# The first 256 tokens as two blocks of 128, the low halves of eight weight chunks through one PSUM bank, and joint maxima of two heads

## The chip, the cores and the metric

The kernel runs on one core of one Trainium2 chip. The metric is the device time of one execution in microseconds. The kernel before took 636.36 us, the median of three runs from 635.49 to 637.52. Beside these stands one more execution, recorded by the profiler, from which all rows below come: 633.81 us, with a span of 632.0 us from its first to its last instruction.

## The reference

Attention with rotated queries and keys, and behind it two matrix products with a bent line between them. Batch 4, 8 heads, 576 tokens, 64 columns a head; then 2304 tokens of 512 columns, 2048 hidden.

```python
def rotate(x):
    x1, x2 = (x[..., :half], x[..., half:])
    return np.concatenate([x1 * cos - x2 * sin, x1 * sin + x2 * cos], axis=-1)
q_rot, k_rot = (rotate(q), rotate(k))
scores = 1.0 / np.sqrt(D) * np.matmul(q_rot, k_rot.transpose(0, 1, 3, 2))
attn = np.exp(scores - np.max(scores, axis=-1, keepdims=True))
attn = attn / (np.sum(attn, axis=-1, keepdims=True) + 1e-09)
x = np.matmul(attn, v)      # heads side by side: 2304 x 512
h = x @ w_in                # 2304 x 2048
g = np.where(h >= 1, h, np.where(h <= -1, 0.0, (h + 1) ** 2 / 4.0))
return g @ w_out            # 2304 x 512
```

The weights come to the kernel as float64 words, q, k and v as float32.

## The kernel before

**Numbers.** Every operand of a matmul is held as two fp16 tiles, a high half and a low half (the rest after rounding). A product is the sum of three: high by high, high by low, low by high (TERMS). The high half is one ScalarE copy, the low half one VectorE instruction that multiplies, subtracts the high half and rounds.

**Attention.** Tokens of a batch go in tiles of 128; a batch has four such tiles and 64 tokens left over. An item is one tile of one pair of heads. For each item TensorE writes the scores of the two heads, 576 columns each, into psS0 and psS1 (L582, 12 matmuls; two PSUM banks each). VectorE takes the maximum of each (L556), ScalarE the exponential with its sum (L558), ScalarE and VectorE scale the sums and take the reciprocal (L561, L563), ScalarE writes the high half of the probabilities (L566) and VectorE the low half (L568). One transposing DMA from SP's queue turns both halves of both heads (phl to pT). When two items of a head pair have landed, 28 matmuls multiply 256 tokens with the values and write psV (L611): the high half of V (vS), the chunk left over and the halves mixed for it (vM, which three DMAs fill from vS), the low half, and zeros (vZ). Two head pairs fill the bank; ScalarE and VectorE read it into the high and low half of xT (L626, L629). After four head pairs the 256 tokens are ready for the MLP. The 64 tokens left over go the same way in items of their own (L594), into xL, and those of two batches make one MLP block of 128 tokens.

**MLP.** A block of 256 tokens takes eight steps. A step is two groups of 12 matmuls of 256 columns into psH (L692), ScalarE's clipped copy a (L699), r and g on VectorE and ScalarE (L702 to L713), and 12 matmuls of 512 columns that add to psO0 and psO1, one bank for each 128 tokens (L722). A block of 128 tokens takes four steps of four groups of 12 at 128 columns and 12 matmuls into one of the two banks. In the first three blocks (ACT_BLOCKS) ScalarE takes over one VectorE instruction in each step.

**Preparation.** Per batch the rows of K and Q are loaded twice (the second time with the halves of the columns swapped), turned with three VectorE instructions (L341, L343, L345), and split. V is scaled with a factor that a root gives: TensorE sums columns with a matmul against ones (L311), and a few small VectorE instructions follow. The weights come in eight chunks of w_in and eight of w_out, 1 MB each. A chunk is decoded by three VectorE instructions (L506, L508, L510) into a float32 scratch of 128 x 1024, which is in turn xT1 and the output tile o; ScalarE writes the high half (L519). For the first five chunks of both (PE_CHUNKS) the low half is made on TensorE, in two half chunks of 512 columns: the scratch through the identity (L535) and minus the high half (L536) into psO0 for the first half chunk and psO1 for the second, from where ScalarE writes it (L539). For the last three it is one VectorE instruction (L527).

**Order.** A planner fixes the order of each engine ahead of time. Each step has a cost in ns, a place in the program and the buffers that it reads and writes; the due times of TensorE's steps go back through what they need, a table SLACK shifts groups of steps and single ones, and the planner lets each engine take, of the steps that are ready by its own clock, the one that is due first. The engines then run their lists in order and wait on semaphores. Loads and transposes stand in SP's list, the later weight chunks in GpSimd's.

## Time and profile before

| | |
|---|---|
| median of three runs | 636.36 us (635.49 to 637.52) |
| profiled execution | 633.81 us, span 632.0 us |
| TensorE busy | 559.8 us, 89% of the span |
| VectorE busy | 511.2 us, 81% |
| ScalarE busy | 441.0 us, 70% |
| GpSimd busy | 7.5 us, 1% |
| read from HBM | 40.96 MB, 72 GB/s with the writes |

Three more kinds of view are used below. A window gives each engine's busy time in a stretch. A timeline gives the rows of one engine in order, with the idle time ahead of a row and what ended it in brackets; the recorded lengths of neighbouring rows overlap a little, so the time that an instruction takes from its engine is read from start to start. A list of waits sums such idle time by the instruction that waited and by what it waited for. A name as psO stands for both tiles of that name in these views.

### The profile page before, as it was taken

The page shows a single profiled execution, that of the slowest core. Times are in us where ns is not written, and L with a number is a line of the kernel's source. Part 1 is how long each engine was busy: PE and PEld are TensorE (multiplying, and loading weights), DVE is VectorE, ACT ScalarE, POOL GpSimd, SP SyncE. Part 2 cuts the span into 40 slices and gives each one's busy share as a digit, 9 for nine tenths or more (in the row PEclk, how much of TensorE's full clock was granted, in tenths as well). Part 3 has the DMA queues.
Part 4 walks back from the last instruction along what each step waited for, and adds up shares of the span by engine and source line. Part 5 has one row for each costly group of instructions (what it writes and reads, how often), then busy time and mean ns, then how long its engine had stood idle before and what let it go on. Part 6 is the DMA issues. An engine that isn't in the chain of part 4 may idle for free.

```text
span 632.0 us, 12652 instructions
## 1 busy us (share of the span) xinstructions
PE 559.8 (89%) x5078; PEld 358.6 (57%) x5078; DVE 511.2 (81%) x839; ACT 441.0 (70%) x881; POOL 7.5 (1%) x18
## 2 busy tenths in 40 slices
PE   1346678799997999999998999999999999999995
PEld 1112234566654666666665676676666676666663
DVE  5998999999999999998897889889877874333422
ACT  3647898978999799984878798877787663232221
POOL 0000100000000000000000000000000000000000
PEclk9997879999998999999999999999999999999999
DMA  8997988695699858876377765856666553000000
GB/s 265 372 305 261 258 231 161 133 233 132 142 260 203 195 99 188 205 164 161 92 163 129 124 127 109 136 94 115 113 131 129 85 99 77 1 8 27 1 34 18
DMA packets 188011, 91.33 MB, mean 145 GB/s; under 512 B 170160, under 2 KB 178608, under 8 KB 185904
## 3 DMA queue, kind: packets, MB, share of 16 engines
q1 hardware_dynamic: 186224, 77.94, 56.0%
q0 software_dynamic: 1728, 12.58, 5.6%
q8 instruction: 40, 0.66, 0.4%
q14 instruction: 19, 0.16, 0.1%
HBM read 40.96 MB, written 4.72 MB: 72 GB/s over the span
## 4 chain that ended last, share of the span: by engine, by line
PE 56%; DVE 22%; DMA 12%; ACT 6%; issue 3%; SPq 0%; ACTq 0%
PE psO L722 21%; PE psH L692 21%; PE psV L611 7%; PE psS L582 5%; DMA pT<-phl 5%; DVE phl L568 4%; DVE mx L556 3%; DMA rk<-in_km_dram 3%; DMA vM<-vS 2%; ACT p L558 2%; DVE g L713 1%; ACT phl L566 1%; DMA rv<-in_vm_dram 1%; DVE r L709 1%; DVE xT L508 1%
## 5 line engine op out<-in xcount | busy, mean ns | idle before, releaser
L722 PE MATMUL psO<-w,g 128*128 128x512 f16 x864 | 211.7, 380 | 1.9 <-ACT g L711 0.9
L692 PEld LDWEIGHTS <-w 128*128 128x128 f16 x1920 | 170.9, 98 | 44.4 <-issue 5.2
L692 PE MATMUL psH<-xT,w 128*128 128x256 f16 x1536 | 187.7, 273 | 3.2 <-ACT a L699 3.2
L558 ACT ACTIVATE p<-psS,mx 128x576 f32<-128x576 f32 x144 | 105.3, 733 | 26.1 <-DVE mx L556 20.1
L722 PEld LDWEIGHTS <-g 128*128 128x128 f16 x864 | 79.3, 98 | 75.2 <-DVE g L713 2.5
L568 DVE SCALAR_TENSOR_TENSOR phl<-p,sums,phl 128x576 f16<-128x576 f32 x144 | 113.4, 812 | 9.6 <-ACT phl L566 9.6
L566 ACT ACTIVATE phl<-p,sums 128x576 f16<-128x576 f32 x144 | 105.0, 765 | 17.5 <-DVE sums L563 15.2
L556 DVE TENSOR_REDUCE mx<-psS 128x1 f32<-128x576 f32 x144 | 104.3, 750 | 6.9 <-PE psS L582 6.2
L582 PE MATMUL psS<-kT,qT 64*128 64x512 f16 (+1 forms) x768 | 64.5, 295 | 22.6 <-ACT p L558 15.3
L711 ACT ACTIVATE g<-r 128x512 f16<-128x512 f32 x72 | 44.9, 624 | 47.5 <-DVE r L709 29.2
L699 ACT ACTIVATE a<-psH 128x512 f32<-128x512 f32 x72 | 42.4, 590 | 49.3 <-PE psH L692 48.7
L713 DVE SCALAR_TENSOR_TENSOR g<-r,g 128x512 f16<-128x512 f32 x72 | 49.5, 688 | 26.8 <-ACT g L711 26.7
L582 PEld LDWEIGHTS <-qT 64*128 64x128 f16 x768 | 31.2, 97 | 68.5 <-issue 47.9
L702 DVE SCALAR_TENSOR_TENSOR r<-a 128x512 f32<-128x512 f32 x48 | 33.1, 689 | 45.6 <-ACT a L699 45.2
L611 PE MATMUL psV<-pT,vS 128*64 128x256 f16 (+1 forms) x768 | 50.1, 253 | 3.8 <-DMA pT<-phl 3.5
L709 DVE SCALAR_TENSOR_TENSOR r<-a,r 128x512 f32<-128x512 f32 x72 | 49.6, 689 | 0.9
L611 PEld LDWEIGHTS <-vS 128*64 128x64 f16 x768 | 33.3, 112 | 18.5 <-issue 14.7
L611 PE MATMUL psV<-pT,vM 128*64 128x256 f16 (+1 forms) x480 | 29.2, 253 | 3.3 <-DMA vM<-vS 3.3
L558 ACT ACTIVATION_READ_ACCUMULATOR p<-psS,mx 128x1 f32 x144 | 28.1, 195 | 0.0
L692 PE MATMUL psH<-xL,w 128*128 128x128 f16 x384 | 25.5, 219 | 0.0
L611 PEld LDWEIGHTS <-vM 128*64 128x64 f16 x480 | 22.0, 113 | 4.1 <-DMA vM<-vS 3.8
L535 PE MATMUL psO<-xT,xL 128*128 128x512 f32 x20 | 15.4, 864 | 9.8 <-DVE xT L510 5.6
(98 smaller groups left out, 467.5 us busy)
## 6 DMA issues: line engine op xcount, KB each, us to landing
w<-in_w_in_dram POOLq DMA_DIRECT2D x5, 1024.0 KB, 6.9
rv<-in_vm_dram SPq DMA_DIRECT2D x8, 512.0 KB, 5.7
w<-in_w_out_dram POOLq DMA_DIRECT2D x4, 1024.0 KB, 7.3
out_dram<-o SPq DMA_DIRECT2D x16, 256.0 KB, 2.4
rq<-in_qm_dram SPq DMA_DIRECT2D x7, 512.0 KB, 7.2
dup<-in_qm_dram SPq DMA_DIRECT2D x7, 512.0 KB, 3.9
dup<-in_km_dram SPq DMA_DIRECT2D x6, 576.0 KB, 5.3
rk<-in_km_dram SPq DMA_DIRECT2D x6, 576.0 KB, 6.8
```

The lines of the kernel that those rows point to most:

```text
L556: plan.add("dve", dve_cost(S, psum=True), at, lambda m=m, src=src: nc.vector.tensor_reduce(out=m, in_=src, op=ALU.max, axis=AX.X, negate=T ...
L558: plan.add("act", act_cost(S, psum=True, ptrs=2), at, lambda a=a, e=e, m=m, src=src: nc.scalar.activation(out=p32[e], in_=src, func=AF.Exp ...
L566: plan.add("act", act_cost(S), at, lambda a=a, e=e, hi=hi: nc.scalar.activation(out=hi, in_=p32[e], func=AF.Copy, scale=rr[:, a:a + 1]), r ...
L568: plan.add("dve", dve_cost(S, ptrs=1), at, lambda a=a, e=e, hi=hi, lo=lo: nc.vector.scalar_tensor_tensor(out=lo, in0=p32[e], scalar=rr[:, ...
L582: nc.tensor.matmul(out=psS[a][:, lo:hi], lhsT=qT[hf][d, l, j, c:c + 128], rhs=kT[ks][d, j, m, lo:hi], start=z == 0, stop=z == 2)
L611: nc.tensor.matmul(out=outs[a], lhsT=st, rhs=moving(a, blk), start=z == 0, stop=z == len(seq) - 1)
L692: nc.tensor.matmul(out=psH[:, n * i:n * i + n], lhsT=wi[ft // 2][:, wl, kk, 128 * (ft % 2):128 * (ft % 2) + 128], rhs=xfn(xl, kk), start=z ...
L699: plan.add("act", act_cost(512, psum=True, ptrs=0), at, lambda one=one: nc.scalar.activation(out=a, in_=psH, func=AF.Relu, scale=2.0 ** -7 ...
L709: plan.add("dve", dve_cost(512), at, lambda one=one: nc.vector.scalar_tensor_tensor(out=r, in0=a, scalar=one, in1=r, op0=ALU.max, op1=ALU. ...
L711: plan.add("act", act_cost(512, ptrs=0), at, lambda g=g, one=one: nc.scalar.activation(out=g[:, 0], in_=r, func=AF.Relu, scale=1.0, bias=- ...
L713: plan.add("dve", dve_cost(512), at, lambda g=g, one=one: nc.vector.scalar_tensor_tensor(out=g[:, 1], in0=r, scalar=-one, in1=g[:, 0], op0 ...
L722: nc.tensor.matmul(out=psO[pos[tt]], lhsT=g[:, gl, n * i + 128 * tt:n * i + 128 * tt + 128], rhs=wo[ft // 2][:, wl, ft % 2, :], start=ft = ...
```

## The change

**Blocks.** The first 256 tokens of batch 0 are two blocks of 128 tokens. Each has four items, four value products of 128 columns that fill the psV bank together, one xT high half and one low half of 512 columns (L618, L621 in the new numbering, into the two halves of xT0), and an MLP block of four steps with groups at 128 columns. The later blocks stay at 256 tokens.

**Weights.** PE_CHUNKS goes from 5 to 8: the low halves of all eight chunks of w_in and of w_out are made on TensorE (L525, L526) and written by ScalarE (L529), and no chunk uses VectorE for it. That is 32 half chunks in place of 20. All of them use psO1 alone.

**Maxima.** psS0 and psS1 are the two halves of one tile. One VectorE instruction takes the maxima of both heads of an item (L545), 2 x 576 elements, in place of two; both exponentials wait for it. Items left over keep one head each.

**Plan.** ACT_BLOCKS goes from 3 to 4, which is the same 24 steps as before, since the first block has become two of four steps. The planner's costs of a score item, of value products and of the first loads change, and the SLACK table is another, so that the order of the whole program is another.

```diff
-    "k0.03 dve": -18_500, "k1 act": 68_700, "k1 dve": 128_000, "k1.12 dve": 2_700, "k1.20 dve": 192_800,
...
+    "k0 dve": 9_000, "k0.02 dve": 20_100, "k0.03 dve": 279_800, "k1 act": 69_500, "k1 dve": 575_900,
...
-PE_CHUNKS = 5
-ACT_BLOCKS = 3
+PE_CHUNKS = 8
+ACT_BLOCKS = 4
...
-    mx = [[sbt(f"mx{i}_{a}", [128, 1]) for a in range(2)] for i in range(4)]
+    mx = [sbt(f"mx{i}", [128, 2]) for i in range(4)]
...
-    psS = [ps.tile([128, 1024], F32, name=f"psS{i}") for i in range(2)]
+    psS_t = ps.tile([128, 2048], F32, name="psS")
+    psS = [psS_t[:, 1024 * i:1024 * i + 1024] for i in range(2)]
...
-                nc.tensor.matmul(out=psO[e], lhsT=idn, rhs=y[:, cut], start=True, stop=False)
-                nc.tensor.matmul(out=psO[e], lhsT=ndg[which], rhs=hi[:, cut], start=False, stop=True)
+                nc.tensor.matmul(out=psO[1], lhsT=idn, rhs=y[:, cut], start=True, stop=False)
+                nc.tensor.matmul(out=psO[1], lhsT=ndg[which], rhs=hi[:, cut], start=False, stop=True)
...
+        srcs = psS_t.rearrange("p (a s) -> p a s", a=2)[:, :, 0:S] if nh == 2 else psS[slot][:, 0:S]
+        plan.add("dve", dve_cost(nh * S, psum=True), at, lambda: nc.vector.tensor_reduce(
+            out=mx[ri][:, 0:nh], in_=srcs, op=ALU.max, axis=AX.X, negate=True),
+            r=[("psS", slot + a) for a in range(nh)], w=[("mx", ri)])
         for a, e in enumerate(es):
-            m, src = mx[ri][a], psS[slot + a][:, 0:S]
-            plan.add("dve", dve_cost(S, psum=True), at, lambda m=m, src=src: nc.vector.tensor_reduce(
-                out=m, in_=src, op=ALU.max, axis=AX.X, negate=True), r=[("psS", slot + a)], w=[("mx", ri, a)])
+            m, src = mx[ri][:, a:a + 1], psS[slot + a][:, 0:S]
...
-        xs = ring("xT", 2)
+        xs = 0 if n == 128 else ring("xT", 2)
+        c0 = 128 * ts[0] if n == 128 else 0
...
-                    dst = [xT[xs][:, l, :, 0:128] for l in range(2)]
+                    dst = [xT[xs][:, l, :, c0:c0 + 128] for l in range(2)]
...
-    blocks = [(b, ts, i == 1) for b in range(B) for i, ts in enumerate(([0, 1], [2, 3]))]
+    blocks = [(b, ts, ts[-1] == T - 1) for b in range(B) for ts in (([0], [1], [2, 3]) if b == 0 else ([0, 1], [2, 3]))]
+    counts["xT"] = 1
```

Three places of the new order, as the instruction lists of the two kernels show them; a number behind a name tells tiles apart.

VectorE ahead of the xT low half that completes the first block, in the kernel before (L629 writes it, for the second two head pairs of 256 tokens; L556 are maxima, L568 probability low halves, L508 and L510 decode a weight chunk into o or xT1):

```order
L556 TENSOR_REDUCE mx1_0_102<-psS0_112 128x1
L556 TENSOR_REDUCE mx1_1_103<-psS1_113 128x1
L568 SCALAR_TENSOR_TENSOR phl0_74<-p32_2_73,sums0_108,phl0_74 128x576
L508 SCALAR_TENSOR_TENSOR xT1_79<-w_61,xT1_79 128x1024
L629 SCALAR_TENSOR_TENSOR xT0_78<-psV_114,sca_99,xT0_78 128x512
L563 RECIPROCAL sums1_109<-sums1_109 128x2
L510 SCALAR_TENSOR_TENSOR xT1_79<-w_61,xT1_79 128x1024
```

and in the kernel after (L621 writes it, for four head pairs of 128 tokens; L545 is a joint maximum, L496 and L498 decode, L555 is the reciprocal):

```order
L555 RECIPROCAL sums2_106<-sums2_106 128x2
L545 TENSOR_REDUCE mx3_103<-psS_108 128x2
L496 TENSOR_SCALAR xT1_79<-w_61 128x1024
L621 SCALAR_TENSOR_TENSOR xT0_78<-psV_109,sca_99,xT0_78 128x4x128
L498 SCALAR_TENSOR_TENSOR xT1_79<-w_61,xT1_79 128x1024
L560 SCALAR_TENSOR_TENSOR phl0_74<-p32_0_71,sums2_106,phl0_74 128x576
```

This low half was instruction 171 of VectorE's list and is 140; the one of the second block is 184. The first turn of the next K (L341 before, L331 after), which was instruction 97, is 168.

TensorE at half chunks of the weights. The kernel before, among the scores of the first items (L535 the scratch through the identity, L536 minus the high half):

```order
L535 MATMUL psO0_116<-xT1_79,xL_80 128x512
L536 LDWEIGHTS xL_80
L536 MATMUL psO0_116<-w_61,xL_80 128x512
L535 MATMUL psO1_117<-xT1_79,xL_80 128x512
L536 LDWEIGHTS xL_80
L536 MATMUL psO1_117<-w_61,xL_80 128x512
```

and the kernel after, at one that stands inside the first MLP block (L685 is its psH group, L715 its product into psO0):

```order
L685 LDWEIGHTS w_61
L685 MATMUL psH_110<-xT0_78,w_61 128x128
L525 MATMUL psO1_112<-xT1_79,xL_80 128x512
L526 LDWEIGHTS xL_80
L526 MATMUL psO1_112<-w_61,xL_80 128x512
L715 LDWEIGHTS g0_83
L715 MATMUL psO0_111<-w_61,g0_83 128x512
```

Half chunks that took psO0 and psO1 in turn take psO1 each time. In the kernel before all 20 half chunks stand ahead of the first MLP matmul; now 15 stand ahead of it and 17 between it and the first MLP matmul of the second block.

TensorE at the first change of batch, where the root of the next V is taken (L311 before, L301 after, 128x3 into psV). The kernel before:

```order
L582 LDWEIGHTS qT0_64
L582 MATMUL psS1_113<-kT1_63,qT0_64 128x64
L311 MATMUL psV_114<-ssv_97,ones_95 128x3
L692 LDWEIGHTS w_61
L692 MATMUL psH_115<-xT1_79,w_61 128x256
```

and the kernel after:

```order
L715 LDWEIGHTS g1_84
L715 MATMUL psO1_112<-w_61,g1_84 128x512
L301 MATMUL psV_109<-ssv_97,ones_95 128x3
L715 LDWEIGHTS g0_83
L715 MATMUL psO0_111<-w_61,g0_83 128x512
```

The root stood behind the last left-over value product and a score item, with two MLP groups and their product behind it; it now stands between two MLP products, and more MLP steps stand between it and the next value product.

## Rows read from the trace of the kernel before

**Rows 1.** The slices of the profile's page: the busy share of TensorE and of VectorE, in tenths, in 40 equal slices of 15.8 us.
```profile
PE   1346678799997999999998999999999999999995
...
DVE  5998999999999999998897889889877874333422
```

**Rows 2.** Windows: a stretch, its length, the busy time of TensorE, of its weight loads, of VectorE, ScalarE and GpSimd in it (with instructions), the mean granted TensorE clock, the DMA share and GB/s.
```profile
0.00:108.70 108.70, 57.16 (x318) 26.85 (x318) 96.82 (x185) 74.67 (x147) 5.41 (x14) 0.92 0.90 266
108.70:186.00 77.30, 71.18 (x673) 46.97 (x668) 76.94 (x112) 67.83 (x131) 2.10 (x4) 1.00 0.76 179
186.00:209.00 23.00, 18.23 (x173) 11.41 (x172) 21.42 (x42) 20.19 (x41) 0.00 (x0) 0.85 0.97 214
```

**Rows 3.** Timeline of TensorE around the first MLP matmul: start, length by the record, line, operation, tiles.
```profile
105.52 1.13 PE L535 MATMUL psO<-o,xL 128*128 128x512 f32 x2
...
106.70 1.02 PE L535 MATMUL psO<-o,xL 128*128 128x512 f32 x2
...
107.87 0.91 PE L582 MATMUL psS<-kT,qT 64*128 64x512 f16 x12
108.71 2.79 PE L692 MATMUL psH<-xT,w 128*128 128x256 f16 x24
```

**Rows 4.** Timeline of VectorE at the turn of the next K (first row; in brackets the idle time ahead of it and what ended it), and ahead of the first MLP matmul.
```profile
50.47 1.36 DVE L341 TENSOR_TENSOR rk<-rk,rt 128x1152 f32<-128x1152 f32 x1 [2.60 <-DMA rk<-in_km_dram]
...
97.68 1.54 DVE L568 SCALAR_TENSOR_TENSOR phl<-p,sums,phl 128x576 f16<-128x576 f32 x2
99.13 1.42 DVE L556 TENSOR_REDUCE mx<-psS 128x1 f32<-128x576 f32 x2
100.46 0.68 DVE L506 TENSOR_SCALAR o<-w 128x1024 uint32<-128x1024 uint32 x1
...
101.67 1.22 DVE L508 SCALAR_TENSOR_TENSOR o<-w,o 128x1024 uint32<-128x1024 uint32 x1
102.80 0.16 DVE L563 RECIPROCAL sums<-sums 128x2 f32<-128x2 f32 x1
...
107.98 0.74 DVE L629 SCALAR_TENSOR_TENSOR xT<-psV,sca,xT 128x512 f16<-128x512 f32 x1
```

**Rows 5.** The chain that ended last, in order of time: start, length, engine, tile, line and instructions in a row. First from the stretch behind the first change of batch, then from the end.
```profile
210.69 1.30 PE psO L722 x6
...
214.22 1.65 PE psV L611 x28
...
217.27 1.31 PE psH L692 x12
...
607.37 1.34 PE psH L692 x24
...
624.15 2.35 PE psO L722 x10
```

**Rows 6.** Timeline of TensorE at the first change of batch: a left-over value product (its first of four rows, with the row behind the last), the column sums for the root of the next V, and the first use of a vM copy.
```profile
187.35 0.32 PE L611 MATMUL psV<-pT,vS 128*64 128x64 f16 x8
...
187.92 0.91 PE L582 MATMUL psS<-kT,qT 64*128 64x512 f16 x12
189.13 0.39 PE L311 MATMUL psV<-ssv,ones 128*128 128x3 f32 x2 [0.31 <-DVE xL L629]
...
202.13 1.28 PE L611 MATMUL psV<-pT,vM 128*64 128x256 f16 x10 [1.55 <-DMA vM<-vS]
```

**Rows 7.** Groups of instructions, different shapes apart: line, engine, operation, tiles, shapes and count; busy us and mean ns of one; idle time ahead of them and what ended it.
```profile
L692 PEld LDWEIGHTS <-w 128*128 128x128 f16 x1920 | 170.9, 98 | 44.4 <-issue 5.2
...
L558 ACT ACTIVATE p<-psS,mx 128x576 f32<-128x576 f32 x144 | 105.3, 733 | 26.1 <-DVE mx L556 20.1 <-DVE phl L568 4.3 <-PE psV L611 0.9
...
L556 DVE TENSOR_REDUCE mx<-psS 128x1 f32<-128x576 f32 x144 | 104.3, 750 | 6.9 <-PE psS L582 6.2 <-PE psS L594 0.6
...
L539 ACT ACTIVATE w<-psO,sca 128x512 f16<-128x512 f32 x20 | 13.1, 677 | 0.8 <-PE psO L536 0.8
...
L519 ACT ACTIVATE w<-xT,sca 128x1024 f16<-128x1024 f32 x8 | 9.1, 1143 | 5.3 <-DVE xT L510 4.1 <-DVE sca L328 1.1
...
L341 DVE TENSOR_TENSOR rk<-rk,rt 128x1152 f32<-128x1152 f32 x6 | 8.1, 1350 | 2.6 <-DMA rk<-in_km_dram 2.6
...
L527 DVE SCALAR_TENSOR_TENSOR w<-xT,sca,w 128x1024 f16<-128x1024 f32 x3 | 3.8, 1280 | 0.2 <-ACT w L519 0.2
...
L341 DVE TENSOR_TENSOR rk<-rk,rt 128x576 f32<-128x576 f32 x4 | 3.0, 755 | 0.0
```

**Rows 8.** What TensorE waited for: line and releaser, us in total, times, the longest. Three rows from 108 to 345 us, and the last one over the whole span.
```profile
PE psS L582 <- ACT p L558: 4.8, 7, 1.5
PE psV L611 <- DMA vM<-vS: 3.3, 2, 1.7
PE psH L692 <- ACT a L699: 3.2, 3, 1.5
...
PE psO L535 <- ACT w L539: 4.3, 5, 2.8
```

**Rows 9.** DMA issues: tile, queue, kind and count, median us from issue to landing.
```profile
pT<-phl SPq DMA_TRANSPOSE x80, 4.6
```

**Rows 10.** Windows of one engine: VectorE's busy time from the start to 232.8 us, and TensorE's from 232.6 us to its last matmul.
```profile
0.00:232.80 232.80, 218.77 (x369) 0.95 0.84 220
...
232.60:626.50 393.90, 389.62 (x3709) 1.00 0.50 101
```

More of the change, by code (lines that the diff above doesn't have):

```diff
@@ L292, in scalar, with dma @@
         return sca[:, nsca[0] - 1:nsca[0]], ("sca", nsca[0])
-    def dma(at, dst, src, r, w, nbytes, eng="sp", chain=[]):
+    def dma(at, dst, src, r, w, nbytes, eng="sp", chain=[], rate=320.0):
         q = nc.sync if eng == "sp" else nc.gpsimd
-        plan.add(eng, 600.0 if eng == "sp" else 1000.0, at, lambda: q.dma_start(out=dst, in_=src), r, w + chain, bw=nbytes / 400.0)
+        plan.add(eng, 600.0 if eng == "sp" else 1000.0, at, lambda: q.dma_start(out=dst, in_=src), r, w + chain, bw=nbytes / (rate if plan.group in ("init", "first") else 400.0))
     def dmaT(at, dst, src, r, w, nbytes):
```

89 lines of the change are left out of this document (39 added, 50 removed).

## The prediction

> **What bounds the kernel now.** I read the slices first [rows 1]: TensorE works a third of the time or less in the first 30 us and from some 110 us on nearly all of the time, with two slices of seven tenths; VectorE is full from the second slice to about the middle. So the kernel is TensorE's work behind a front in which VectorE feeds it too slowly. The windows give the sizes [rows 2]: ahead of 108.7 us TensorE is busy 57.2 us, partly at a reduced granted clock (0.92 in the mean), while VectorE is busy 96.8; behind it TensorE idles 6.1 of 77.3, then 4.8 of 23.0 (at a granted clock of 0.85). The edge at 108.7 is the first MLP matmul [rows 3]: it starts when the second xT low half of the first 256 tokens is done, which VectorE ends at the same moment.
>
> Prices are taken start to start. A VectorE instruction begins 0.08 ahead of the recorded end of the one before (101.67 plus 1.22 against 102.80) [rows 4], so each costs its row less 0.08. TensorE's pieces: one L692 group of 12 at 256 columns 1.31, at 128 columns 0.67, three L722 matmuls 0.65, a value product 1.65, for a left-over item 0.57, a score item 0.84, one half chunk through the identity 1.18 (105.52 to 106.70) [rows 3, 5, 6]. At these prices all of TensorE's pieces make 529.1 us. 40.4 lie ahead of 108.7, 488.7 behind.
>
> All differences are made on the profiled execution (633.81, span 632.0) and put on the median of the three runs, 636.36.
>
> **The change, part by part.**
>
> *Split first block.* The first MLP matmul now needs four items and four value products, not eight and four. The order has 19.9 us less on VectorE ahead of the xT low half that completes the first block: 20 single maxima (13.4) against 8 joint ones (10.2), 12 against 18 probability low halves (-4.4), 25 against 32 decode steps (-6.9), no turn of the next K (three of 1.27, -3.8), and 1.6 of small ones [rows 4, 7]. It also leaves out the one VectorE wait of size, 2.6 us for the next K at 50.47 [rows 4]: that turn now stands at row 168, some 45 us of VectorE work later, with its load issued before the first transposes. The first MLP matmul so moves from 108.7 to 108.7 - 19.9 - 2.6 = 86.2.
>
> *TensorE's added work.* 12 half chunks of 1.18 make 14.2. 64-column and 256-column value products give 0.57 and 1.65 and bound the 128-column one; on the line between them it is 0.93, so eight cost 7.4 in place of 6.6 (bounds 4.6 to 13.2). 32 MLP groups of 0.67 replace 16 of 1.31: 0.4. Sum +15.5 (544.6 in all); 29.1 of it lies ahead of the first MLP matmul, 515.5 behind. Start plus work behind goes from 108.7 + 488.7 = 597.4 to 86.2 + 515.5 = 601.7: **4.3 us worse, unless TensorE waits less behind that point.**
>
> *VectorE and ScalarE.* Six low halves (L527) leave VectorE, 1.20 each: -7.2. ScalarE takes 12 evictions of 0.68 less its overlap of 0.09: +7.1; it idles 34 us ahead of 108.7 and 9.5 in the 77 behind [rows 2], which hides them; without that cover they cost 7.1. No row shows a joint maximum. 576 more elements cost 0.595 (0.755 to 1.350) [rows 7], so it takes 0.75 + 0.595 = 1.345, 1.26 start to start, against 1.33 for a pair [rows 4]: 0.07 saved in each of 64. Bounds: 1.19 (no fixed part) and 1.42 (the pair's recorded length), -9.0 to +5.8 over the kernel, under half of that ahead of the point below. Its first exp starts 0.6 later; TensorE waited for an exp 7 times between 108 and 345 us [rows 8], so that is 0 to 4.2. I take 0, since those waits stand where the order has changed, and keep 4.2 for the range. The Trainium skill (VectorE: DVE Perf Modes, The TRN2 errata) gives a PSUM-source instruction a fixed 120 cycles at 0.96 GHz, 0.125 us: by it the 64 save 8.0 in place of 4.5. The pair that takes 1.33 in this trace speaks for less.
>
> *Queues.* SP's first 28 issues are the same. Then loads of K, Q and the three vM copies stand ahead of the first transposes, which wait for VectorE anyway; I cost it at nothing, covered by the 16 us of VectorE work between the fourth item's last low half and the xT behind it; without it a transpose's landing of 4.6 us [rows 9] is late. The half chunks share one bank: each waits for ScalarE's eviction of the one before, and TensorE's whole queue waits behind it. Ahead of 86 us TensorE has over 50 us to spare; behind it see the second rival.
>
> *Where the waits go.* After 108.7 TensorE has idle rows of 4.8 (exp), 3.3 (vM) and 3.2 us (ScalarE's read of psH) [rows 8]. The largest spot is the change of batch: at 189.13 the column sums for the root that scales the next V are taken, and TensorE stands on the last vM copy until 202.13 [rows 6]. That is 13 us, and in the order TensorE has 6.9 us of pieces there; its clock falls to 0.85 for the window [rows 2]. The new order has 19.5 us of pieces between that root and the next value product (18.2 against 16.1 at the second change of batch, 10.4 against 8.7 at the third). This spot should vanish.
>
> *What VectorE still allows.* At each MLP step and value product I added VectorE's work up to its input and TensorE's pieces from it on. The largest sum before is the 15th MLP step, 219.0 + 0.2 + 379.1 = 598.3; the window to 232.8 confirms the first number, 218.8 busy and 14.0 idle [rows 10]. The largest now is the 21st value product: 219.0 + 9.5 (eight more K and Q turns) - 7.2 (L527) - 0.5 (maxima) + 2.8 (two more low halves, one more MLP step, small ones) = 223.6, and 5.0 for transposing and landing, and 369.5 of pieces: 598.1. The sums are equal. So VectorE sets the pace up to there in both, and the change can win only in what lies above the sum.
>
> **The sum.** Before: TensorE takes from 232.6 to its end at 626.5 [rows 5, 10] 393.9 us for 379.1 of pieces, a factor of 1.039 that holds 4.3 us of idle time (393.9 less 389.6); 5.5 us of eviction and output follow. Now: 223.6 + 5.0 + 11.4 (14.0 idle less the 2.6) = 240.0, then 369.5 x 1.039 = 383.9, then 5.5: 629.4. If the idle time goes too: 625.2. I take the middle, 627.3, 4.7 under 632.0: **636.4 - 4.7 = 631.7 us**. By way of the first MLP matmul the end is 8.3 us earlier (74.1 of VectorE's work ahead of the first block's xT low half, 0.2 and 515.5 make 589.8 against 598.1): TensorE's slack in the front.
>
> **Rivals.** *No change.* VectorE waits for something else in the place of K and the waits at the change of batch turn up at another edge: the sums alone differ by 0.2, so 636.2. For it: ScalarE is busy 88% of the stretch behind 108.7 and gets more; against it: the longer cover at all three changes of batch.
>
> *Slower: the single bank.* Between the first MLP matmul and the second block's first one stand 47 us of pieces with 17 half chunks, one each 2.8 us. If ScalarE's eviction ends more than 1.6 us after the matmuls (2.8 - 1.2), TensorE stands. An eviction of 0.68 behind one exp (0.73) and one 1024-wide copy (1.14) [rows 7] ends after some 2.6 us: 17 x 1.0 = 17 us, less the slack of 8.3, is +8.7, and the time 640.4. It decides for slower from 2.5 us on. For it: ScalarE's queue is in order and full. Against it: with two banks the 20 half chunks of the present kernel waited for evictions five times, 4.3 us in all and 2.8 at the longest [rows 8]. At that rate 17 wait 3.7 us, inside the slack; only if most are like the longest does the rival come.
>
> *Narrow matmuls.* If the weight load of 98 ns [rows 7] set the pace of the 384 matmuls at 128 columns, they would cost 16.1 more, 7.8 after the slack: 639.5. Against it stand 24 such matmuls in 1.34 us, 56 ns each [rows 5], with the same weights. The Trainium skill (TensorE: Matmul & The Clock Gate, Back-to-back issue gap) has such pairs sustained at about 81 ns, a rule that speaks against narrow blocks; by it the change costs 9.6 more, 1.3 after the slack, and the time is 633.0. The row decides for 56.
>
> **How the numbers follow.** A measurement of this kernel can tell about 0.3%, 1.9 us, from no change. My forecast 0.57 (with its own range 626 to 634.4), no change 0.23, the single bank 0.14, narrow matmuls 0.03, more than forecast (VectorE's joint maxima at their lower bound) 0.03. Faster 0.58, same 0.23, slower 0.19. For 8 in 10 the range reaches down to 625 (joint maxima 2 better, all waits gone and less idle) and up to 640.5 (the single bank, or the waits for exps and value products of 1.65 together).
>
> **What will show it.** The first L685 matmul at 84 to 90 us; 12 of them at 128 columns in 0.67; a joint maximum of 1.30 to 1.40 us; VectorE idle 10 to 13 us ahead of 240; no wait for vM at the first change of batch; waits of L525 for ScalarE under 5 us behind the first MLP matmul. Wrong would be: TensorE idle over 12 us between 90 and 240, above all ahead of L525, or VectorE idle over 16 us in the same stretch.

## The result and the profile after

The changed kernel takes 643.09 us (median of eight runs, 640.88 to 647.68), the kernel before 635.30 in the same runs. The ratio is 1.0128 with a 95% interval of 1.0101 to 1.0155: 1.3%, some 8.1 us, slower. The profiled execution took 647.68 us, with a span of 645.9; it is the slowest of the eight, 4.6 us above their median, while the one of the kernel before stands 1.5 below its median. So 6 of the 13.9 us between the two traces are scatter and no part of the change; where that matters, the trace of e7 below stands beside it, a form of the changed kernel that took the same time and whose profiled execution (641.22 us) is nearer to the median. Of e5 and e9 below, some executions took over 1.5% longer than the fastest of the same kernel, and these are not compared.

The slices of the page, TensorE and VectorE, to lay beside [rows 1]:

```profile
PE   1238569989989999999989999999999999999996
...
DVE  6988689999999998999977888758668577634322
```

The windows up to the first MLP matmul, to the change of batch and over it (columns as in [rows 2]):

```profile
0.00:92.50 92.50, 43.21 (x267) 20.00 (x268) 76.42 (x150) 59.00 (x116) 4.54 (x13) 0.96 1.01 269
92.50:186.00 93.50, 85.59 (x922) 53.55 (x921) 89.64 (x121) 83.77 (x160) 2.64 (x5) 1.00 0.84 192
186.00:209.00 23.00, 21.90 (x244) 14.18 (x244) 22.73 (x37) 20.58 (x44) 0.00 (x0) 1.00 0.69 143
```

TensorE reaches the first MLP matmul at 92.5 us in place of 108.7, with 43.2 us of work behind it. From there to 186 us it idles 7.9 of 93.5, and over the change of batch 1.1 of 23.0 at full clock, where it had idled 4.8 at 0.85 [rows 2]. The timeline of TensorE, at the first value products, the first MLP matmul, and the first MLP groups behind it:

```profile
59.50 0.41 PE L603 MATMUL psV<-pT,vS 128*64 128x128 f16 x8
...
60.41 1.12 PE L525 MATMUL psO<-xT,xL 128*128 128x512 f32 x2
...
70.94 0.64 PE L603 MATMUL psV<-pT,vS 128*64 128x128 f16 x8 [4.59 <-DMA pT<-phl]
...
91.34 1.12 PE L525 MATMUL psO<-o,xL 128*128 128x512 f32 x2 [1.71 <-ACT w L529]
...
92.51 0.83 PE L685 MATMUL psH<-xT,w 128*128 128x128 f16 x12
...
104.49 1.50 PE L685 MATMUL psH<-xT,w 128*128 128x128 f16 x24
105.83 1.08 PE L525 MATMUL psO<-o,xL 128*128 128x512 f32 x2
```

A value product of 128 columns takes 0.91 (59.50 to 60.41), 24 matmuls of 128 columns 1.34 (104.49 to 105.83), 56 ns each. At 70.94 TensorE had stood 4.6 us on a transpose, and VectorE, one timeline down, 5.6 us on the scratch that TensorE had not yet read:

```profile
74.68 0.69 DVE L496 TENSOR_SCALAR o<-w 128x1024 uint32<-128x1024 uint32 x1 [5.64 <-PE psO L525]
...
91.37 0.74 DVE L621 SCALAR_TENSOR_TENSOR xT<-psV,sca,xT 128x512 f16<-128x512 f32 x1
```

The change of batch: the column sums for the root, and the only wait for vM up to 345 us.

```profile
199.26 0.28 PE L301 MATMUL psV<-ssv,ones 128*128 128x3 f32 x2
...
222.07 0.30 PE L603 MATMUL psV<-pT,vM 128*64 128x256 f16 x2 [0.57 <-DMA vM<-vM]
```

The groups with the joint maxima, the evictions of the half chunks, and the maxima of the items left over (columns as in [rows 7]):

```profile
L545 DVE TENSOR_REDUCE mx<-psS 128x2 f32<-128x1152 f32 x64 | 86.3, 1348 | 3.5 <-PE psS L574 3.4
...
L529 ACT ACTIVATE w<-psO,sca 128x512 f16<-128x512 f32 x32 | 21.8, 680 | 10.0 <-PE psO L526 9.5
...
L545 DVE TENSOR_REDUCE mx<-psS 128x1 f32<-128x576 f32 x16 | 11.8, 748 | 6.1 <-PE psS L586 5.3 <-ACT p L550 0.8
```

What TensorE waited for between 92 and 345 us, against [rows 8]. The waits for vM and psH are shorter than they were. Those of the score items are not: with the items left over (L586), which had no such wait there before, they sum to 5.4 us for exponentials and maxima, where it was 4.8. The wait of the half chunks is new in this stretch:

```profile
PE psO L525 <- ACT w L529: 5.8, 4, 1.9
PE psS L574 <- ACT p L550: 2.9, 3, 2.2
...
PE psH L685 <- ACT a L692: 1.8, 2, 1.1
PE psS L586 <- ACT p L550: 1.7, 4, 0.7
PE psS L586 <- DVE mx L545: 0.8, 1, 0.8
...
PE psV L603 <- DMA vM<-vM: 0.6, 1, 0.6
```

And behind 250 us, first the kernel before (its largest, and the only one of a score item), then the changed kernel (its three largest):

```profile
PE psV L611 <- DMA vM<-vS: 1.7, 1, 1.7
...
PE psS L582 <- ACT p L558: 0.4, 1, 0.4
```

```profile
PE psS L574 <- ACT p L550: 4.4, 5, 2.2
PE psS L586 <- ACT p L550: 3.1, 4, 1.2
PE psS L586 <- DVE mx L545: 1.4, 2, 0.8
```

There the score items wait for exponentials and maxima 8.9 us, where they waited 0.4. Half of it, 4.5 us, is of the items left over (L586).

**Where the time went.** The sum of the prediction was made up to one value product, the 21st (the 17th of the kernel before, for the same tokens). VectorE up to the low half that it waits for, before and after, and TensorE from it to the last matmul, before and after:

```profile
0.00:244.30 244.30, 229.78 (x389) 0.95 0.83 217
```

```profile
0.00:248.60 248.60, 227.14 (x355) 0.99 0.92 218
```

```profile
250.90:626.50 375.60, 371.79 (x3554) 1.00 0.49 99
```

```profile
253.30:641.30 388.00, 377.56 (x3590) 1.00 0.48 93
```

VectorE has 2.6 us less to do there (229.8 to 227.1) and idles 7.0 more (14.5 to 21.5). The value product starts at 253.3 instead of 250.9. From it on, pieces of 369.5 us are left instead of 365.5, and they take 388.0 instead of 375.6: 18.5 over the pieces instead of 10.1. That is 2.4 + 4.0 + 8.4 = 14.8 us to the last matmul; the eviction behind it is 0.9 shorter. The 4.0 are three MLP groups of 12 matmuls. In the trace of e7 VectorE idles 17.4, the product starts at 249.0 and TensorE then takes 385.8:

```profile
0.00:244.00 244.00, 226.64 (x355) 0.97 0.91 222
```

```profile
249.00:634.80 385.80, 377.46 (x3590) 1.00 0.48 93
```

That is -1.9 + 4.0 + 6.2 = 8.3, close to the difference of the medians. **VectorE's part is hardly faster, and behind it TensorE has more left and takes more than its pieces.**

### The profile page after: what moved, and what is told of

The parts are those of the page before. It is cut to its first block, busy times and chain, and to the rows that moved or that the text cites. A ratio compares the mean times of both kernels' runs of the same rounds, so it can differ in the third digit from the quotient of the medians.

```text
span 645.9 us, 13237 instructions
## 1 busy us (share of the span) xinstructions
PE 571.2 (88%) x5418; PEld 364.8 (56%) x5418; DVE 500.9 (78%) x769; ACT 446.5 (69%) x893; POOL 7.2 (1%) x18
## 4 chain that ended last, share of the span: by engine, by line
PE 40%; DVE 5%; DMA 5%; ACT 5%; issue 1%; SPq 0%; ACTq 0%; DVEq 0%
PE psO L715 17%; PE psH L685 16%; PE psS L574 3%; PE psV L603 3%; DMA pT<-phl 3%; ACT p L550 2%; DVE mx L545 1%; ACT phl L558 1%; DVE phl L560 1%; DMA rv<-in_vm_dram 1%; PE psS L586 1%; DMA dup<-in_qm_dram 1%; DVE r L702 0%; ACT g L704 0%; DVE vS L344 0%
## 5 line engine op out<-in xcount | busy, mean ns | idle before, releaser
L715 PE MATMUL psO<-w,g 128*128 128x512 f16 x864 | 213.8, 380 | 1.5 <-ACT g L704 0.9
L685 PEld LDWEIGHTS <-w 128*128 128x128 f16 x2112 | 175.6, 98 | 47.0 <-issue 6.3
L685 PE MATMUL psH<-xT,w 128*128 128x256 f16 (+1 forms) x1728 | 190.0, 261 | 1.9 <-ACT a L692 1.8
L715 PEld LDWEIGHTS <-g 128*128 128x128 f16 x864 | 78.3, 98 | 75.7 <-issue 3.9
L545 DVE TENSOR_REDUCE mx<-psS 128x2 f32<-128x1152 f32 (+1 forms) x80 | 98.1, 1228 | 9.6 <-PE psS L586 5.3
L574 PE MATMUL psS<-kT,qT 64*128 64x512 f16 (+1 forms) x768 | 61.0, 293 | 12.7 <-ACT p L550 11.8
L603 PE MATMUL psV<-pT,vS 128*64 128x256 f16 (+2 forms) x832 | 51.6, 247 | 8.9 <-DMA pT<-phl 7.8
L603 PEld LDWEIGHTS <-vS 128*64 128x64 f16 x832 | 34.8, 112 | 24.2 <-issue 20.3
L603 PE MATMUL psV<-pT,vM 128*64 128x256 f16 (+2 forms) x520 | 29.7, 244 | 0.6 <-DMA vM<-vM 0.6
L529 ACT ACTIVATE w<-psO,sca 128x512 f16<-128x512 f32 x32 | 21.8, 680 | 10.0 <-PE psO L526 9.5
L525 PE MATMUL psO<-o,xL 128*128 128x512 f32 x32 | 19.6, 697 | 8.7 <-ACT w L529 8.7
L685 PE MATMUL psH<-xL,w 128*128 128x128 f16 x384 | 25.9, 219 | 0.0
```

What stands on the lines that cost most here:

```text
L545: plan.add("dve", dve_cost(nh * S, psum=True), at, lambda: nc.vector.tensor_reduce(out=mx[ri][:, 0:nh], in_=srcs, op=ALU.max, axis=AX.X, n ...
L574: nc.tensor.matmul(out=psS[a][:, lo:hi], lhsT=qT[hf][d, l, j, c:c + 128], rhs=kT[ks][d, j, m, lo:hi], start=z == 0, stop=z == 2)
L603: nc.tensor.matmul(out=outs[a], lhsT=st, rhs=moving(a, blk), start=z == 0, stop=z == len(seq) - 1)
L685: nc.tensor.matmul(out=psH[:, n * i:n * i + n], lhsT=wi[ft // 2][:, wl, kk, 128 * (ft % 2):128 * (ft % 2) + 128], rhs=xfn(xl, kk), start=z ...
L715: nc.tensor.matmul(out=psO[pos[tt]], lhsT=g[:, gl, n * i + 128 * tt:n * i + 128 * tt + 128], rhs=wo[ft // 2][:, wl, ft % 2, :], start=ft = ...
```

## The experiments

Each edit is made so that the planner's order stays, unless the text says otherwise. Ratios are to the kernel before in the same runs, with 95% intervals.

**e1: three loads moved behind two transposes.**

```diff
+        sp = [i for i in out if steps[i][0] == "sp"]
+        late = sp[36:39]
+        out = [i for i in out if i not in late]
+        at = out.index(sp[40]) + 1
+        out[at:at] = late
```

> The changed kernel with three loads of SP's queue (K, the left-over V rows, Q of the next part) moved behind the two transposes that stood right behind them at 55.8 us; nothing else moves. Theory queue: that transpose landed 15.1 us after its issue because the three loads lay ahead of it; TensorE then waited 4.6 us for pT at 70.9 us and VectorE 5.6 us for the scratch that TensorE had not read. Without them it lands in 5 to 8 us, the first MLP matmul moves from 92.5 to about 87 us, and if the work behind it sets the end, the time falls by 4 to 5.6 us, to 637.5 to 639. Rival traffic: the 1 MB weight chunks of GpSimd's queue make it late; the landing stays over 12 us and the time at 643. Rival elsewhere: the landing gets shorter and the first MLP matmul earlier, but the time stays within 1.5 us of 643, since later waits give it back.

651.77 us, ratio 1.0264 (1.0230 to 1.0298): slower by 8.7 than the changed kernel. The transposes between 40 and 130 us, issue to landing, first the changed kernel, then e1:

```profile
DMA to landing us min/median/max: 4.7/8.2/15.1
```

```profile
DMA to landing us min/median/max: 4.7/8.6/17.3
```

The long landing went with the loads: they stand now ahead of the next transposes, one of which takes 17.3 us, and VectorE idles there instead, in pieces. A transpose right behind the loads lands late in both; that this wait sets the time is not shown by it.

**e5: the same loads left out.**

```diff
+        sp = [i for i in out if steps[i][0] == "sp"]
+        out = [i for i in out if i not in sp[36:39]]
```

> The changed kernel without the three loads of SP's queue that stand right ahead of the third and fourth transposes (second half of the next batch's K, its left-over V rows, its Q): they are left out, so that the next batch is worked out on rows loaded before, and no transpose has them ahead of it. Theory queue and front: the third transpose lands in 5 to 8 us, TensorE's 4.6 us for pT and VectorE's 5.6 us for the scratch go, the first MLP matmul moves from 92.5 to about 87 us, and the time falls by 4 to 6 us, to 637 to 639. Theory back: the first MLP matmul moves as much, but waits behind it grow by the same, and the time stays within 1.5 us of 643.

641.45 us, ratio 1.0109 (1.0075 to 1.0143), from runs that scatter from 640.4 to 651.4, unexplained. In the profiled one (641.60) the first MLP matmul starts at 90.3. The gain, 1.6 us, lies within the intervals, so the three loads are not the cause of the 8 us. The transpose that had stood behind them now lands after 6.3 us, but a later one, issued at 74.1 us with no load of SP's queue right ahead of it, after 14.4:

```profile
DMA to landing us min/median/max: 4.5/7.3/14.4
```

A weight chunk of 1 MB was issued 1.3 us before it from GpSimd's queue, as one was 1.2 us before a transpose of the changed kernel that landed after 13.6. So the loads on SP's queue are not the only thing that makes a transpose late; whether the weight chunks are was not tried.

**e2: the low halves of the last three chunks back on VectorE.**

```diff
             def rest(e=e, cut=cut):
+                if c >= 5:
+                    return
...
+            def low(e=e, cut=cut):
+                if c < 5:
+                    nc.scalar.activation(out=lo[:, cut], in_=psO[1], func=AF.Copy, scale=f)
+                elif e == 1:
+                    nc.vector.scalar_tensor_tensor(out=lo, in0=y, scalar=f, in1=hi, op0=ALU.mult, op1=ALU.subtract)
```

> The changed kernel with the low halves of the last three chunks of w_in and w_out back on VectorE, one instruction each in the place of the second eviction; 12 half chunks and 12 evictions are left out, the order of all else stays. Theory TensorE: from the first MLP matmul on TensorE's work sets the end, and 12 half chunks of 1.18 us stand there; the time falls by 7 to 14 us, to 629 to 636. Theory VectorE (the prediction's): VectorE's work up to the 21st value product sets the pace; 7.2 us more of it there gives 643 to 650.

648.94 us, ratio 1.0235 (1.0208 to 1.0263): 5.9 slower, with 14.2 us less on TensorE. The 5.9 are not the price of VectorE's 7.2 us alone: the low halves stand where the second evictions stood, and the granted clock of TensorE, 1.00 from 90 to 250 us in the changed kernel, is 0.94 there. TensorE's wait for those low halves is new:

```profile
PE psH L692 <- DVE w L535: 5.1, 2, 4.7
```

**e16: the same low halves left out on every engine**, the products reading high halves in their place.

```diff
             def rest(e=e, cut=cut):
+                if c >= 5:
+                    return
...
+                        nc.tensor.matmul(out=psH[:, n * i:n * i + n], lhsT=wi[ft // 2][:, wl if ft < 10 else 0, kk, 128 * (ft % 2):128 * (ft % 2) + 128],
...
+                                             rhs=wo[ft // 2][:, wl if ft < 10 else 0, ft % 2, :], start=ft == 0 and z == 0, stop=ft == FT - 1 and z == 2)
```

> The changed kernel with the low halves of the last three chunks left out on every engine (12 half chunks of 1.18 us on TensorE, 12 evictions on ScalarE); the MLP products that would read them read the high halves instead, so their number stays. VectorE's work is that of the changed kernel. It prices TensorE's added work alone. Theory TensorE: the end follows TensorE's work from the first MLP matmul on, 9 to 14 us less, 629 to 634. Theory VectorE: VectorE's work up to the 21st value product sets the pace, 0 to 4 us less, 639 to 643.

644.79 us, ratio 1.0136 (1.0069 to 1.0204): with 14.2 us of TensorE's work and 12 evictions taken away there is no gain. A gain of 9 to 14 us is excluded; one of 4 would still lie in the interval. From 90 to 250 us TensorE idles 19.5 us, where the changed kernel idles 11.6; more than half of it is spent on exponentials:

```profile
PE psS L579 <- ACT p L555: 10.5, 4, 5.6
```

It is busy 5.0 of the 9 us from 120 to 129, and then its granted clock falls to 0.52, nearly all at the lower of the two levels (1.2 GHz):

```profile
129.00:136.00 7.00, 5.35 (x22) 2.26 (x23) 7.00 (x9) 4.75 (x10) 0.00 (x0) 0.52 0.62 147
```

In the changed kernel it is busy 8.3 of the same 9 us, and the clock stays at 1.00. So some 8 of the 14.2 us come back as waiting. Some 5 more may have gone to the clock (an estimate: 10.2 us at the lower level between 129 and 143 us, half of it lost if TensorE works all the time), and no run parts the two.

**e17: the six L527 instructions of the kernel before left out**, with the same reading of high halves.

```diff
+            plan.add("dve", dve_cost(1024, ptrs=1), at, lambda: None,
```

> The kernel before with the low halves of the last three chunks left out (6 VectorE instructions of 1.20 us); the MLP products read the high halves instead, their number stays. TensorE's work is that of the kernel before. It prices VectorE's work alone. Theory VectorE: 5 to 7 us less, 627 to 629. Theory TensorE: 0 to 2 us less, 632 to 634.

632.02 us, ratio 0.9964 (0.9941 to 0.9986): 2.3 us for 7.2 of VectorE's. The rest turns into VectorE's waiting. Up to the low half of that value product VectorE has 6.4 us less to do and is done at 244.9, where it was at 244.3; it idles 21.5 us in place of 14.5:

```profile
0.00:244.90 244.90, 223.43 (x383) 0.94 0.82 216
```

So in these two executions VectorE's work up to there doesn't set the pace by itself, full as the engine is: work taken from it comes back as many short waits, the largest new ones of some 1 to 2 us each, mostly for ScalarE and TensorE.

**e3: separate maxima and two score tiles in the changed kernel.**

```diff
-    mx = [sbt(f"mx{i}", [128, 2]) for i in range(4)]
+    mx = [[sbt(f"mx{i}_{a}", [128, 1]) for a in range(2)] for i in range(4)]
...
-    psS_t = ps.tile([128, 2048], F32, name="psS")
-    psS = [psS_t[:, 1024 * i:1024 * i + 1024] for i in range(2)]
+    psS = [ps.tile([128, 1024], F32, name=f"psS{i}") for i in range(2)]
...
+            for a in range(nh):
+                nc.vector.tensor_reduce(out=mx[ri][a], in_=psS[slot + a][:, 0:S], op=ALU.max, axis=AX.X, negate=True)
```

> The changed kernel with two maxima of one head each in the place of the joint one, into tiles of their own, and the score banks as two tiles as before; the order stays. Theory exp: the joint maximum delays an item's first exponential by 0.65 us, and one score tile for both banks makes instructions on one bank wait for those on the other; behind 250 us TensorE waits 11 us for exponentials and maxima where it waited 1 in the kernel before. With separate maxima 4 to 8 us of it go: 635 to 639. Theory VectorE: 64 times 0.07 us more on VectorE give 643 to 647.

640.46 us, ratio 1.0089 (1.0059 to 1.0119): 2.6 faster, at the edge of the noise; e7 and e14 below are the same pair once more, 4.1 apart with intervals that don't meet. **e8: the same separate maxima, but in one score tile** (the second pair of lines above left out).

> The changed kernel with two maxima of one head each in the place of the joint one, the score banks left as halves of one tile. It parts what the joint instruction saves from what the one tile costs. Theory one tile: the time goes up by what two maxima cost more than one joint (64 times 0.07 = 4.5 us on VectorE), 645 to 649, against 640.5 with two tiles; one tile then costs 5 to 8 us in this order. Rival: the one tile costs nothing here, 639 to 642.

645.96 us, ratio 1.0192 (1.0157 to 1.0227). Between e8 and e3 only the tile differs: one tile costs 5.5 us in this order, and the joint instruction gives back 2.9 of them (e8 to the changed kernel). The price is paid behind the front: at the same probability low half e8's trace is 2.0 us ahead of e3's near 278 us and 3.3 behind it near 400. A part of it is TensorE's own. The items left over write the two halves in turn; with two tiles one half is written while the other is still read, with one tile the writing waits. Behind 250 us the score items left over wait in e8 for exponentials, 2.7 us, and for maxima, 1.4 us, and in e3 not at all, where the other score items' wait is all:

```profile
PE psS L589 <- ACT p L553: 2.7, 3, 1.2
```

```profile
PE psS L576 <- ACT p L552: 2.1, 4, 1.1
```

**e6: one score tile in the kernel before, nothing else.**

```diff
-    psS = [ps.tile([128, 1024], F32, name=f"psS{i}") for i in range(2)]
+    psS_t = ps.tile([128, 2048], F32, name="psS")
+    psS = [psS_t[:, 1024 * i:1024 * i + 1024] for i in range(2)]
```

> The kernel before with its two score tiles as halves of one, and separate maxima as they were. Theory one tile: instructions on one half wait for those on the other, and a good part of the 9.9 us of the joint maxima in the kernel before come from that; 637 to 640. Theory joint instruction: the one tile costs nothing, within 1.5 us of 634.5, and the 9.9 us come from the first exponential's later start.

649.22 us, ratio 1.0233 (1.0205 to 1.0261): **15.3 us for a change of two lines that compute nothing.** **e4: joint maxima on top of it**, in the place of the first of each two.

```diff
...
+            def maxima(a=a):
+                srcs = psS_t.rearrange("p (a s) -> p a s", a=2)[:, :, 0:S] if nh == 2 else psS[slot][:, 0:S]
+                if a == 0:
+                    nc.vector.tensor_reduce(out=mx[ri][:, 0:nh], in_=srcs, op=ALU.max, axis=AX.X, negate=True)
```

> The kernel before with joint maxima in the place of the first of each two, and one tile for the score banks; the order of all else stays. Theory exp: TensorE waits longer for exponentials, +3 to +6 us: 638 to 641 where the kernel before has 635. Theory VectorE: 4.5 us less on the engine that sets the pace, up to the 15th MLP step, -2 to -4.5: 631 to 633.

644.25 us, ratio 1.0161 (1.0135 to 1.0187): 9.9 us slower than the kernel before, so the joint instruction takes some 5 of the 15.3 back. How one tile costs that much is read from the timeline. The kernel before, where the first exponential starts while the second maximum runs:

```profile
485.03 1.42 DVE L556 TENSOR_REDUCE mx<-psS 128x1 f32<-128x576 f32 x2
485.82 0.74 ACT L558 ACTIVATE p<-psS,mx 128x576 f32<-128x576 f32 x1 [1.62 <-DVE mx L556]
```

and e6, where it starts when both are done, and where a second maximum that stands behind a first exponential waits for that one:

```profile
509.62 1.41 DVE L557 TENSOR_REDUCE mx<-psS 128x1 f32<-128x576 f32 x2
...
511.13 0.74 ACT L559 ACTIVATE p<-psS,mx 128x576 f32<-128x576 f32 x1 [1.61 <-DVE mx L557]
...
516.43 0.74 ACT L559 ACTIVATE p<-psS,mx 128x576 f32<-128x576 f32 x1 [0.97 <-DVE mx L557]
...
517.29 0.76 DVE L557 TENSOR_REDUCE mx<-psS 128x1 f32<-128x576 f32 x1 [0.30 <-ACT p L559]
```

The second maximum and the first exponential read different banks, and still one waits for the other's engine: with one tile the program's semaphores put its readers on two engines in a row. The traces show how. In both, 44 pairs of maxima stand back to back. In the kernel before the first exponential starts before the second maximum has ended in 34 of them, in e6 in none: there the first maximum of such a pair updates no semaphore, and the second one signals for both. The sums of the waits, ScalarE's for maxima (kernel before, then e6) and VectorE's for exponentials, which the kernel before doesn't have:

```profile
ACT p L558 <- DVE mx L556: 20.1, 24, 1.9
```

```profile
ACT p L559 <- DVE mx L557: 39.8, 45, 2.5
```

```profile
DVE mx L557 <- ACT p L559: 5.6, 7, 1.9
```

**e7: the first 14 half chunks in two banks.**

```diff
-                nc.tensor.matmul(out=psO[1], lhsT=idn, rhs=y[:, cut], start=True, stop=False)
+                nc.tensor.matmul(out=psO[e if i < 7 else 1], lhsT=idn, rhs=y[:, cut], start=True, stop=False)
...
```

> The changed kernel with the first 14 half chunks, all ahead of the first MLP matmul, in psO0 and psO1 in turn in place of psO1 alone; the order stays. Theory bank (the prediction's second rival): the waits for the eviction of the half chunk before, 12.4 us of which some 8 stand ahead of the first MLP matmul, hold VectorE's scratch and with it the front; 2 to 4 us less, 639 to 641. Theory no bank: TensorE has time to spare there, within 1.5 us of 643.

642.56 us, ratio 1.0128 (1.0098 to 1.0158): no difference. **e14: e3 and e7 together.**

> The changed kernel with separate maxima in two score tiles and the first 14 half chunks in two banks: the two edits that took 2.6 and 0.5 us alone. If they add up, 639 to 641; the kernel before stays ahead.

638.44 us, ratio 1.0066 (1.0038 to 1.0095); against e3 within the intervals. Its profiled execution (636.19, the fastest of the five) shows the front nearly as the prediction had it: the first MLP matmul at 87.1, and VectorE idle 11.9 us up to the low half at 239.8.

```profile
87.12 0.83 PE L687 MATMUL psH<-xT,w 128*128 128x128 f16 x12
```

```profile
0.00:239.80 239.80, 227.95 (x382) 0.98 0.91 226
```

It is the fastest form of the change that was run, and still 4.1 us behind the kernel before.

**Parts alone, planned again.** An attempt to part split and chunks. e12 is the kernel before with PE_CHUNKS = 8 and its own table; e13 has split, eight chunks in psO1 and that table; e9 is the kernel before with `SLACK = {}`, e10 that with the split, e11 with the split and eight chunks in psO1, e15 with the split, five chunks, all in psO1.

> The kernel before, its table and its blocks of 256, with the low halves of all eight chunks through TensorE in both banks; planned with the old table. It parts the eight chunks from the split. Theory VectorE: 7.2 us less of it in the stretch that it bounds give 627 to 631. Theory bank: the first block's product into psO0 and psO1 has to wait for the last half chunks in both, and with blocks of 256 nothing can stand in between: 640 to 655.

> The kernel before with its old table, the split first block and all eight chunks in psO1, and with separate maxima in two score tiles. Theory one tile: the changed kernel lost by its one score tile and its joint maxima, and split and chunks alone are no slower than the kernel before: 630 to 637 (if the old table fits as well). Theory work: the 15 us more on TensorE behind an earlier start cost about what they cost in the changed kernel with separate maxima, 6 us: 638 to 646. Over 650 it would tell of the table only.

> The kernel before with an empty SLACK table, so that the planner's costs alone set the order. It is the base for the next two, in which no table favours either side. Theory order: the table is worth 5 to 20 us, 640 to 655. Rival: it is worth little, within 2 us of 634.

> As the run before (kernel before, empty SLACK table), with the first 256 tokens as two blocks of 128; separate maxima, two score tiles, five chunks through two banks. Theory split pays: the first MLP matmul comes 10 to 20 us earlier and the time falls by 2 to 6 us against the run before. Theory no gain: TensorE waits behind it as much more, and 1 to 3 us of added work show: within 3 us or slower.

> As the run before, with the low halves of all eight chunks through TensorE in psO1. Theory VectorE (from the five-chunk run): VectorE loses 7.2 us of work in the stretch that it bounds, and the time falls by 3 to 7 us against the run before. Theory TensorE: 14.2 us more of TensorE's work give 5 to 14 us more.

> Empty table, split first block, five chunks, but all half chunks in psO1. Against the run without a table with the split and both banks (685) it tells what the second bank cost there, against the one with eight chunks (659) what the three chunks bring. Theory bank: most of the 27 us between those two are the first block's product waiting for psO0; 660 to 668. Theory VectorE: most are the low halves on VectorE; 675 to 685.

e12: 658.35 us, ratio 1.0389 (1.0331 to 1.0447). The first MLP groups start at 104.7, but the first product into psO0 and psO1 stands behind the last half chunks, until 144.6:

```profile
104.74 2.78 PE L692 MATMUL psH<-xT,w 128*128 128x256 f16 x24
...
144.61 0.81 PE L722 MATMUL psO<-w,g 128*128 128x512 f16 x3 [0.99 <-ACT w L539]
```

So with blocks of 256, in this order, the first block's product has no bank until the last chunk is through: the split, which leaves psO1 free during the first block, is what makes room for them. e13: 663.38, ratio 1.0456 (1.0437 to 1.0475), a table that doesn't fit. e9: 663.74 with runs from 647 to 669, so no base to compare with; e10: 685.35, ratio 1.0812; e15: 667.91, ratio 1.0513; e11: 658.64, ratio 1.0385. In these plans without a table the second bank costs the split 17.4 us (e10 to e15), and the three chunks on TensorE bring 9.3 (e15 to e11), the direction that e2 had; each of them is an order of its own. What the split alone does can't be read from a base that scatters by 22 us.

## Why the prediction was wrong

The forecast was 631.7 us in a range of 625.0 to 640.5; it took 643.1. The terms of its sum, all up to the low half of the 21st value product and from there, beside three traces (the changed kernel's is its slowest execution, e14's its fastest):

| us | VectorE's work | its idle time | to the product | start of the product | TensorE to its end | rest | span |
|---|---|---|---|---|---|---|---|
| forecast | 223.6 | 11.4 | 5.0 | 240.0 | 383.9 | 5.5 | 629.4 |
| changed kernel | 227.1 | 21.5 | 4.7 | 253.3 | 388.0 | 4.6 | 645.9 |
| e7 | 226.6 | 17.4 | 5.0 | 249.0 | 385.8 | 4.6 | 639.4 |
| e14 | 228.0 | 11.9 | 5.6 | 245.4 | 384.4 | 4.6 | 634.4 |

**The step that failed is "14.0 idle less the 2.6" under "VectorE sets the pace up to there".** It counts every microsecond taken from VectorE as a microsecond of time and holds VectorE's waits at what they were. The start of the 21st product, put at 240.0, measured 253.3, and 249.0 in e7: 6 to 10 us of that are idle time, 3 to 3.5 work. e17 shows the same in the kernel before: 7.2 us of VectorE's work left out bring 2.3 us of time (0.9 to 3.7 by the interval), and in its trace the low half is done no earlier, with 7.0 us more of waiting. The second failure is the score tile, which the sum has at nothing. It costs time behind that point, where the forecast has the idle time of the kernel before or less. Step by step:

- *The first MLP matmul at 86.2*: 92.5 in the profiled run, 87.1 in e14, 90.3 and 90.9 in e5 and e7. The term was right in kind, and some 4 to 6 us too good: VectorE's wait of 2.6 us for K is gone, but one of 5.6 for the scratch came (until 74.7 us), behind a transpose that landed 15.1 us after its issue. VectorE idles 16.1 us ahead of that matmul, where it idled 11.9. The step "I cost it at nothing" on SP's loads missed it; e1 and e5 move or remove the loads and with them that landing, and no gain beyond the intervals comes of it.
- *TensorE's added work*: the prices held (0.91 for a value product against 0.93, 56 ns a narrow matmul). That the 14.2 us of half chunks are covered fits e16, with the clock as an open part of it.
- *Narrow matmuls*: a rival that did not come. The Trainium skill (TensorE: Matmul & The Clock Gate, Back-to-back issue gap) gives some 81 ns for such a pair, and the row at 104.49 has 56; the measurement decides.
- *The change of batch*: right. The wait for vM fell from 3.3 to 0.6 us, and the clock stayed up.
- *The single bank*: the waits behind the first MLP matmul were 5.8 us, above the bound of 5 and inside the slack of 8.3. e7 changes only the half chunks ahead of that matmul. For those behind it stands e16, where these waits are 1.6 us and the time is no better. The rival's time, 640.4, was near the result by another cause.
- *Joint maxima*: the duration was right (1.348 against 1.345). The tile that the joint instruction needs was not costed at all. In the kernel before, tile and instruction cost 9.9 us (e4), the tile alone 15.3 (e6); in the changed order, made for them, the tile costs 5.5 (e8 to e3) and both together 2.6 (e3) or 4.1 (e7 to e14). "Its first exp starts 0.6 later ... I take 0" can't be priced by itself, since no run has the joint instruction without the one tile; with that tile the instruction saves time. The prediction looked for the price among waits that stood ahead of 345 us; behind 250 us, where the kernel before had TensorE full (0.4 us of waits for exponentials), the changed kernel waits 8.9, and 4.5 of them are of the items left over, which no term had.
- *"The sums are equal ... the change can win only in what lies above the sum"*: the sum was 3 us too low, 227.1 + 4.7 + 369.5 = 601.3 against 598.1, mostly in VectorE's work: between the two windows the trace has four more probability low halves and two more MLP steps, where the count has two and one. Above the sum the forecast took 2.6 us less of VectorE's idle time and some 2 us less of TensorE's; the traces of the changed kernel and e7 have 3 to 7 more of the one, and TensorE takes 6 to 8 us more over its pieces than it did, with 4.0 more of pieces behind the same value product.
- *The signs*: neither of the two for being wrong came. Between 90 and 240 us TensorE idles 11.6 us (12 was the sign) and VectorE 5.3 (16). Most of VectorE's waits stand ahead of 92 us and the new ones of the score items behind 250, outside the stretch that was named. The sign that did tell is VectorE's idle time ahead of 240 us, 21.4 where 10 to 13 was named.

Shown by runs: the tile with the joint instruction (2.6 to 4.1 of the some 8 us), that less work on VectorE is not as much less time (e17), that the half chunks' 14.2 us don't add to the time, that the bank of the first 14 half chunks and the three loads are not the cause. The other 4 to 5 us are not settled: they lie in the new order's front (VectorE's idle time, 11.9 to 21.5 between executions and forms of this kernel), in the 4.0 us of pieces that it leaves behind the 21st product, and in what TensorE then takes over its pieces. Which waits make up VectorE's idle time is read from the traces; that any one of them sets the time is not shown. No run parts the split from the order, since each new plan without a fitted table moves the front by more than the effect.

## What to carry to other kernels

Work added to an engine that waits in a stretch cost no time here that the runs could show, and work taken from the engine that is full in a stretch is worth only what does not turn into its waiting: 2.3 us of 7.2. A sum of work with the old idle time added to it is therefore not yet a forecast: ask which waits take the place of the work. Before two buffers become one tile so that one instruction can read both, count what the program then puts in a row: readers of the two halves on different engines, and the writer of one half behind the readers of the other. Look over the whole span, above all where the engine that waits is full.

## What the runs showed that was not expected

One score tile in place of two, with the same instructions and order, costs 15.3 us (a ratio of 1.0233); ScalarE's waits for maxima go from 20.1 us in 24 to 39.8 in 45, and VectorE waits for exponentials 5.6 us in 7, which it had never done. The instructions themselves take as long as before (a maximum 748 ns against 750, an exponential 735 against 733), so this is the order that the program's semaphores put on the users of one tile, and no slower reading. A transposing DMA issued right behind loads of 0.5 MB landed after 15.1 and 17.3 us, where the median of the kernel before is 4.6 [rows 9]; but one without such loads right ahead of it landed after 14.4 (e5). And a joint maximum of 1152 columns saves 0.148 us of recorded length on two of 576 (2 x 0.748 less 1.348), of which only 0.06 count start to start: the Trainium skill (VectorE: DVE Perf Modes, The TRN2 errata) gives the fixed part as 120 cycles at 0.96 GHz, an estimate of 0.125 us, with which the recorded lengths roughly agree; the overlap of 0.08 between neighbours takes the larger part of it away.
